# Batch-walking tiles, loads that cast in the DMA, crossbar transposes and a planner with explicit buffers in a fused attention and feed-forward kernel

## Chip, cores and metric

One core of one Trainium2 chip. The metric is the device time of one execution in microseconds. The profile is one execution of the same program, taken on the chip. In the profile PE is the matrix engine (PEld its weight loads), DVE the vector engine, ACT the scalar engine, POOL the GpSimd engine and SP the sync engine, which here only issues DMAs.

## The reference

Attention over 4 batches, 8 heads, 768 positions and head size 64, where a query sees the first 8 keys (global) and the last 96 (local), with a bias linear in the distance. The heads are joined and go through two products with `h - tanh(h)` between them.

```python
scores = q @ k.T / sqrt(64)                      # per batch and head
keep   = (key < 8) | ((0 <= query - key) & (query - key < 96))
dist   = where(global and not local, 96, |query - key|)
a      = softmax(where(keep, scores - slope[h] * dist, -1e9))
x      = (a @ v), heads joined                   # 3072 x 512
h      = x @ w_in                                # 3072 x 2048
out    = (h - tanh(h)) @ w_out                   # 3072 x 512, fp32
```

A tile is 128 query positions of one batch, all heads; there are 24 tiles, six per batch. A tile needs only its own keys, those of the previous tile of its batch, and the 8 global ones, which are copied into unused columns of the previous tile's keys.

## The kernel before

The program first describes every piece of work as an operation with an engine, an estimated duration, what it must come after and which buffers it takes and gives back. A planner then simulates these and emits the instructions of each engine in the order that the simulation found. At run time each engine keeps that order, and semaphores guard the data.

The parts that matter (the cuts are marked):

```python
# tiles u = 0..23 go along batch 0, then batch 1, ...; u // NQ is the batch
def load(u, nm, src, dst):                       # fp32, 256 KB, in rows of 256 bytes
    b, i = u // NQ, u % NQ
    dst[u] = stpool.tile([P, H, Dh], FP32, name=nm)
    started(("ld", nm, u), nc.sync.dma_start(out=dst[u], in_=src[b, :, i*P:(i+1)*P, :]...))
def cast(u, nm, src, dst, eng):                  # POOL (DVE for tile 0): fp32 -> bf16
    dst[u] = bpool.tile([P, H * Dh], BF16, name=nm)
    eng.tensor_copy(out=dst[u], in_=src.pop(u)...)
# ... [cut]
before = [("t", 0), ("t", 1), ("t", 2), ("in", 0), ("t", 3), ("in", 1), ("in", 2), ("in", 3),
          ("out", 0), ("out", 1), ("t", 4), ("out", 2), ("out", 3), ("t", 5)]
for n, it in enumerate(before):                  # loads of tiles wait for loads of weights and the reverse:
    if n >= 2 and (it[0] == "t") != (before[n - 1][0] == "t"):
        gate_of[("ld", "kf", it[1]) if it[0] == "t" else it] = landed(before[n - 2])
# ... [cut]
def a_T(u):                                      # 8 PE transposes of k and q, then a DVE copy
    tr[u] = ps_sm.tile([P, 2, NP, P], BF16, name="sm")
    for j, src in ((1, k_bf), (0, q_bf)):
        for p in range(NP):
            nc.tensor.transpose(tr[u][:, j, p, :], src[u][:, p*P:(p+1)*P], ident)
def a_X(u):                                      # 4 PE transposes of x, then a DVE copy
    ...
groups = [[0, 1], [2, 3], [4, 5]] + [[u, u+1, u+2] for u in range(6, NU, 3)]   # first product
```

The weights come in eight casting DMAs issued by POOL, four quarters of `w_in` and four of `w_out`. PSUM is three pairs of banks (scores and first product) and two single banks (transposes, weighted values, second product).

The softmax here doesn't subtract the row's maximum and nothing guards it: scores larger than these inputs give would overflow.

## Time and profile before

| | before |
|---|---|
| time, median of 2 runs | 243.35 us |
| PE busy, DVE, ACT, POOL | 90%, 60%, 46%, 27% |
| the chain that ended last | PE 85% |
| last weight quarter issued, then to landing | 38.55 us, 7.8 us later (46.4 us) |

This is the profile page of the kernel before: busy time by engine, then the busy share of each engine in 40 equal slices in tenths, the granted PE clock, and the DMA engines.

```profile
span 242.5 us, 4763 instructions
PE 217.6 (90%) x1926; PEld 133.8 (55%) x1952; DVE 144.9 (60%) x274; ACT 111.0 (46%) x137; POOL 66.0 (27%) x111
...
PE   1477867999999979999999999999999999999994
...
PEclk9999799999999999999999999999999999999999
DMA  8997998999999998580991161101100101111112
...
PE 85%; DVE 5%; ACT 3%; DMA 2%; issue 2%; SPq 1%; POOL 1%; ACTq 0%; POOLq 0%
```

One digit of the rows is 6.1 us. PE is full from the eighth digit on, so what can be won lies in the work itself or in the first 45 us, where the DMA row is nearly full: the kernel waits for data.

A busy PE is not a measure of work done, because matmuls overlap and the granted clock changes (0.50 for 3.4 us in the kernel before). So I count the recorded matmuls up to a time and price each with its spacing in warm stretches of the timeline (first product 0.109 us per 256 columns, 0.1625 per 384; second product 0.2165; a transpose 0.0575; a score 0.030; weighted values 0.031). Time minus work done is what PE has lost by then. It is an estimate. Some traces miss up to 29 matmul records, all of the second product and spread evenly, and are scaled up for them; differences below 1 us are not to be read. (The figures here are a recount on which work, losses and the tail add up to the span. The recorded texts below use an earlier count, which has up to 1.2 us more work done by 50 us.)

### The profile page before, as it was taken

How to read it: one execution, taken by the hardware profiler on the slowest of the kernel's cores; microseconds unless marked ns; L12 is line 12 of the kernel's file. 1: busy time of each engine (PE TensorE's matmuls, PEld its weight loads, DVE VectorE, ACT ScalarE, POOL GpSimd, SP SyncE). 2: the span in 40 equal slices, each digit the busy share in tenths (PEclk: the TensorE clock that was granted, in tenths of full speed). 3: DMA queues.
4: the chain of work that ended last, by engine and by line, in shares of the span. 5: the costliest groups of instructions: out<-in, count | busy, mean ns of one | idle time of the engine just before them, and what ended most of it. 6: DMA issues, size and time to landing. Idle time of an engine off the chain costs nothing.

```text
span 242.5 us, 4763 instructions
## 1 busy us (share of the span) xinstructions
PE 217.6 (90%) x1926; PEld 133.8 (55%) x1952; DVE 144.9 (60%) x274; ACT 111.0 (46%) x137; POOL 66.0 (27%) x111
## 2 busy tenths in 40 slices
PE   1477867999999979999999999999999999999994
PEld 1354565655685456646555656665555655555541
DVE  1464474855489558967976677569447866334300
ACT  4443072625257336724862474367325752334310
POOL 5628206156436225432511215130110110000000
PEclk9999799999999999999999999999999999999999
DMA  8997998999999998580991161101100101111112
GB/s 157 218 216 114 203 219 130 217 223 210 260 236 232 207 251 205 97 188 31 221 214 46 35 142 43 43 3 43 44 26 19 46 0 46 45 43 46 43 43 87
DMA packets 82581, 29.66 MB, mean 122 GB/s; under 512 B 75392, under 2 KB 79488, under 8 KB 82560
## 3 DMA queue, kind: packets, MB, share of 16 engines
q1 hardware_dynamic: 78336, 25.17, 47.3%
q0 software_dynamic: 4224, 4.19, 11.0%
q8 instruction: 15, 0.25, 0.4%
q14 instruction: 6, 0.05, 0.1%
HBM read 27.26 MB, written 6.29 MB: 138 GB/s over the span
## 4 chain that ended last, share of the span: by engine, by line
PE 85%; DVE 5%; ACT 3%; DMA 2%; issue 2%; SPq 1%; POOL 1%; ACTq 0%; POOLq 0%
PE big L263 35%; PE op L292 32%; PE big L184 5%; PE sm L172 5%; DMA qf<-in_q_dram 2%; PE sm L207 2%; PE sm L239 2%; DVE g L282 2%; ACT ot L302 1%; PE sm L212 1%; PE sm L292 1%; SPq L147 1%; DVE x L225 1%; ACT th L275 1%; POOL q_bf L160 1%
## 5 line engine op out<-in xcount | busy, mean ns | idle before, releaser
L275 ACT ACTIVATE th<-big 128x768 f32<-128x768 f32 (+1 forms) x60 | 51.3, 855 | 84.9 <-PE big L263 83.8
L282 DVE TENSOR_TENSOR g<-big,th 128x768 bf16<-128x768 f32 (+1 forms) x60 | 60.5, 1009 | 25.0 <-ACT th L275 24.7
L292 PEld LDWEIGHTS <-g 128*128 128x128 bf16 x384 | 34.5, 98 | 35.1 <-issue 1.9
L192 ACT ACTIVATE pd<-big 128x1024 bf16<-128x1024 f32 x24 | 24.5, 1021 | 11.8 <-PE big L184 11.8
L160 POOL CAST k_bf<-kf 128x512 bf16<-128x512 f32 x23 | 16.4, 712 | 36.7 <-PE sm L172 23.3
L263 PE MATMUL big<-xT,w_in_bf_98 128*128 128x384 bf16 (+1 forms) x144 | 24.6, 321 | 0.6 <-DVE xT L246 0.6
L292 PE MATMUL op<-w_out_bf_102,g 128*128 128x512 bf16 x82 | 23.1, 379 | 2.2 <-ACT ot L302 1.5
L263 PE MATMUL big<-xT,w_in_bf_99 128*128 128x384 bf16 (+1 forms) x144 | 24.8, 324 | 0.0
L302 ACT COPY ot<-op 128x512 f32<-128x512 f32 x23 | 13.5, 588 | 24.1 <-PE op L292 22.4
L263 PE MATMUL big<-xT,w_in_bf_100 128*128 128x384 bf16 (+1 forms) x144 | 23.1, 308 | 1.3 <-ACT pd L192 1.3
L292 PE MATMUL op<-w_out_bf_103,g 128*128 128x512 bf16 x88 | 23.1, 379 | 0.2
L176 DVE COPY qk<-sm 128x1024 bf16<-128x1024 bf16 x24 | 16.5, 688 | 11.2 <-PE sm L172 11.1
L263 PE MATMUL big<-xT,w_in_bf_101 128*128 128x384 bf16 (+1 forms) x144 | 23.1, 308 | 0.1
L292 PE MATMUL op<-w_out_bf_105,g 128*128 128x512 bf16 x87 | 22.7, 379 | 0.5 <-issue 0.2
L292 PE MATMUL op<-w_out_bf_104,g 128*128 128x512 bf16 x85 | 22.5, 379 | 0.7 <-issue 0.5
L192 ACT ACTIVATE po<-big 128x1024 bf16<-128x1024 f32 x20 | 20.5, 1026 | 1.5 <-PE big L184 1.5
L224 DVE RECIPROCAL rden<-sm 128x4 f32<-128x4 f32 x40 | 7.2, 180 | 20.9 <-PE sm L212 17.7
L207 PEld LDWEIGHTS <-pd 128*128 128x128 bf16 x192 | 14.6, 101 | 7.7 <-DVE x L225 3.8
L196 DVE TENSOR_TENSOR pd<-pd,mk 128x1024 bf16<-128x1024 bf16 x24 | 17.0, 710 | 2.9 <-ACT pd L192 2.9
L263 PEld LDWEIGHTS <-w_in_bf_98 128*128 128x128 bf16 x144 | 14.1, 102 | 8.1 <-issue 0.9
L263 PEld LDWEIGHTS <-w_in_bf_99 128*128 128x128 bf16 x144 | 14.4, 103 | 6.9
L263 PEld LDWEIGHTS <-w_in_bf_100 128*128 128x128 bf16 x144 | 13.7, 98 | 8.2 <-issue 1.2
(106 smaller groups left out, 250.4 us busy)
## 6 DMA issues: line engine op xcount, KB each, us to landing
kf<-in_k_dram SPq DMA_DIRECT2D x24, 256.0 KB, 4.8
qf<-in_q_dram SPq DMA_DIRECT2D x24, 256.0 KB, 4.9
vf<-in_v_dram SPq DMA_DIRECT2D x24, 256.0 KB, 4.8
out_dram<-ot SPq DMA_DIRECT2D x24, 256.0 KB, 2.1
w_in_bf_98<-in_moe_w_in_dram POOLq DMA_DIRECT2D x1, 512.0 KB, 5.6
w_in_bf_99<-in_moe_w_in_dram POOLq DMA_DIRECT2D x1, 512.0 KB, 5.4
w_in_bf_100<-in_moe_w_in_dram POOLq DMA_DIRECT2D x1, 512.0 KB, 7.3
w_in_bf_101<-in_moe_w_in_dram POOLq DMA_DIRECT2D x1, 512.0 KB, 9.2
```

Of the source, the lines that this page charges most:

```text
L160: eng.tensor_copy(out=dst[u], in_=src.pop(u).rearrange("p h d -> p (h d)"))
L172: nc.tensor.transpose(tr[u][:, j, p, :], src[u][:, p * P : (p + 1) * P], ident)
L176: nc.vector.tensor_copy(out=qk[u], in_=tr.pop(u))
L184: nc.tensor.matmul(s[:, slot(2 * p + hh), :], qk[u - o][r, 1, p, :], qk[u][r, 0, p, :], start=True, stop=True,)
L192: nc.scalar.activation(pr[u, o], s, AF.Exp, bias=0.0, scale=scale)
L196: nc.vector.tensor_tensor(out=pr[u, o], in0=pr[u, o], in1=mk[:, :, m, :], op=ALU.mult)
L207: nc.tensor.matmul(t[:, h, :], pr[u, 0][:, slot(h0 + h), :], vb[u % NV][:, h0 + h, :], start=True, stop=last,)
L263: nc.tensor.matmul(t[:, a, o : o + n], w_in_bf[j][:, c, fo : fo + P], xT[g][:, c, 0:n], start=(c == 0), stop=(c == CD - 1),)
L275: nc.scalar.activation(h_view(ths[g, f0], g), h_view(hs[g, f0], g), AF.Tanh, bias=0.0, scale=1.0)
L282: nc.vector.tensor_tensor(out=dst, in0=h_view(hs.pop((g, f0)), g), in1=h_view(ths.pop((g, f0)), g), op=ALU.subtract,)
L292: nc.tensor.matmul(os_[u], gs[g][:, f, t * P : (t + 1) * P], w_out_bf[f // FJ][:, f % FJ, :], start=(f == 0), stop=(f == CF - 1),)
L302: nc.scalar.copy(out=ots[u], in_=os_.pop(u))
```

## The change

Its intent: take transposes off PE and casts off POOL, and let the first product begin earlier. The core of the diff (cut; the planner and all operations are rewritten):

```diff
+    tiles = [(u % B, u // B) for u in range(NU)]          # batch, position: four batches at each position
+    HEAD = 4
+    NPE = 6
+    groups = [[u] for u in range(HEAD)] + [[u, u + 1] for u in range(HEAD, NU, 2)]
+    bufs["pair"] = [psum.tile([P, 2, BANK], FP32, ...) for i in range(2)]     # scores, weighted values
+    bufs["bank"] = [psum.tile([P, BANK], FP32, ...) for i in range(4)]        # both products, transposes
-        dst[u] = stpool.tile([P, H, Dh], FP32, name=nm)
-        started(("ld", nm, u), nc.sync.dma_start(out=dst[u], in_=...))
+                    pl.op(key, POOL, 0.75, lambda ...: nc.gpsimd.dma_start(out=dst(), in_=rows(src, u)),   # casts
+                          after=[prev and ("issue", prev), ...], take=take, dma=T_LD, ...)
-            if n >= 2 and (it[0] == "t") != (before[n - 1][0] == "t"):
-                gate_of[...] = landed(before[n - 2])
+            if u < NPE:
+                pl.op(("T", nm, u), PE, 0.24, ...)          # as before, on PE
+            else:
+                pl.op(("T", nm, u), SP, 0.6, lambda ...: nc.sync.dma_start_transpose(
+                          out=bufs[nT][got[tT]], in_=buf(nm + "b", (nm + "b", u))), ..., dma=T_TR, lag=0.5)
+        # ... [cut] x is transposed in the same way: PE for u < NPE, the crossbar for the rest
```

All loads but k and q of tile 0 now stand in one queue, POOL's, with the weights between them; the gates are gone. Tile 4 also moved in front of the first two quarters of `w_out`, and the copies of v's global rows went from POOL to DVE.

## The prediction

> **What bounds it now.** The chain of waits is 85% PE (line 263, first product, 35%; line 292, second product, 32%); PE is busy 90% of 242.5 us. PE's work, estimated from warm stretches of the timeline: second product 16 x 0.2165 us per tile, 83 us; first product 83 (0.1625 us per 384 columns, 0.109 per 256); scores 10.6; weighted values 11; k/q transposes 24 x 0.46 = 11; x transposes 24 x 0.23 = 5.5. Sum about 204.5. So 38 us are lost: counting matmuls per stretch, 27 by 60 us, 31 by 100 us, 3.5 in the remaining 139, and 3.6 after the last matmul (eviction 0.59, store 2.1). The early loss is feed: the DMA row is full to 50 us, loads run at about 218 GB/s, a tile's three loads take 3.6 us and a weight quarter 3.2, so six tiles and eight quarters need about 47 us; and the first-product matmuls at 20 us take 200 ns instead of 109.
>
> **What the change does.**
> 1. Removes PE transposes of 18 of 24 tiles: 18 x 0.69 = 12.4 us of PE, on the chain, so most of it counts; and 18 x 1.1 us of DVE copies (DVE is at 60%, off the chain).
> 2. Replaces them with 54 crossbar transposes of 128 KB. No run shows their time. [...] plus issue and 2 us or more to landing, as the page shows for stores. [...] Off the chain in steady state; a wait is likely at the first crossbar tiles (6 to 8).
> 3. k, q, v are cast in the DMA. [...] 70 POOL casts (0.6-0.7 us) go; 70 issues of 1024 short rows come. The weights' issues (512 rows) took 0.75 us; I expect 0.8 to 1.2. POOL was 27% busy. HBM bytes do not fall, so loads still limit the start.
> 4. Batch walk: the first four tiles have no previous tile and pass the first product singly as weight quarters land. By hand, 27-28 us of PE work is done by 50 us, against 24 before: 2-4 us gained, less 1 for 128-column matmuls.
> 5. Evictions go from 768 to 512 columns: tanh 0.6, subtract 0.69 (extrapolated from the trace). ACT and DVE stay near 50-55%. Four single banks hold both products: 2-4 us more stalls.
>
> **Sum.** 193 (PE work) + 23-26 (start) + 3-5 (crossbar hand-over) + 4-6 (steady) + 3.6 (tail) = about 230 us. Range 221 to 240. Chances: faster 0.80, same 0.13, slower 0.07.
>
> **What will show it.** Matmuls of PE transposes down to a quarter; PE busy near 200 us; 95% or more after 80 us; loads 1.1 to 1.3 us apart at the start; the last weight quarter landing near 47-50 us; crossbar transposes landing in 2-4 us; the tail unchanged. The gain should appear mostly after 60 us.
>
> **What would make it wrong.** Cast loads of 256-byte rows much slower than 218 GB/s, or issues on POOL over 1.5 us [...]; crossbar transposes of several us each, blocking stores behind them on SP's in-order queue and so the three output buffers; bank rotation stalling PE. Each pushes to 240 or beyond. If the start packs better than I count, 220.

The sum came to about 230 us (193 + 24.5 + 4 + 5 + 3.6 with the middles of the ranges). The 3-5 us of hand-over, the 2-4 us to landing and "off the chain in steady state" are estimates. That no issue on POOL would take over 1.5 us was likewise an expectation.

## More of the kernel before

The weights as POOL issued them in the kernel before, with two copies that stood in front of them (start, duration, instruction; in brackets the idle time before it, and what ended it):

```profile
10.36 0.89 POOL L153 DMA_DIRECT2D w_in_bf_98<-in_moe_w_in_dram  x1 [0.27 <-DMA vf<-in_v_dram]
...
18.45 0.61 POOL L231 COPY vb_107<-vb_106 8x512 bf16<-8x512 bf16 x1 [4.39 <-PE op L212]
19.01 0.75 POOL L153 DMA_DIRECT2D w_in_bf_99<-in_moe_w_in_dram  x1
...
37.25 0.61 POOL L231 COPY vb_109<-vb_106 8x512 bf16<-8x512 bf16 x1 [10.68 <-PE op L212]
37.81 0.75 POOL L156 DMA_DIRECT2D w_out_bf_104<-in_moe_w_out_dram  x1
38.55 0.75 POOL L156 DMA_DIRECT2D w_out_bf_105<-in_moe_w_out_dram  x1
```

The gaps between them have two causes. One is the waits of one load for another (the gates): the second quarter of `w_in` waited for the first to land, at 15.96 us, and the third of `w_out` for the second, at 34.96. The other is POOL's order: both stood behind a copy of the global rows of v that waited for PE, and left some 3 us after their gates had opened.

## The result, and the profile after

| | before | after |
|---|---|---|
| median, 2 runs | 243.35 us | 230.22 us |
| ratio, fast runs | 1 | 0.945 (0.938 to 0.952) |
| PE's work in all, of the span | 204.5 of 242.5 us | 192.8 of 228.0 us |
| lost by 40 us | 25.6 us | 17.8 us |
| work done / lost by 50 us | 24.1 / 25.9 us | 29.3 / 20.7 us |
| lost by 70 us | 27.5 us | 21.3 us |
| lost by 90 us | 30.4 us | 28.9 us |
| lost by 140 us, 220 us | 33.4, 34.7 us | 30.5, 31.3 us |

A ratio is the mean time of one kernel's fast runs over that of the other's of the same rounds, so it is not quite the ratio of the medians. The predicted 230.0 us was met. The terms of the sum were not, as the table shows: the start lost less than predicted, and 7.6 us went between 70 and 90 us.

The profile page of the changed kernel (same rows as above):

```profile
span 228.0 us, 5127 instructions
PE 207.8 (91%) x2056; PEld 143.3 (63%) x2056; DVE 128.1 (56%) x250; ACT 120.1 (53%) x192; POOL 71.4 (31%) x96
...
PE   1669699789999589999999999999999999999993
...
PEclk9999999999999959999999999999999999999999
DMA  5999999999999999999999999793422321001112
...
PE 87%; DMA 4%; DVE 3%; POOL 2%; ACT 1%; issue 1%; POOLq 0%
```

The PE row has a dent, a 5, in its fourteenth digit (74 to 80 us), and the clock row a 5 in the fifteenth. The weights in the changed kernel's POOL timeline:

```profile
9.46 0.81 POOL L396 DMA_DIRECT2D w_in_bf<-in_moe_w_in_dram  x1
12.80 2.33 POOL L396 DMA_DIRECT2D w_in_bf<-in_moe_w_in_dram  x3
20.00 1.52 POOL L401 DMA_DIRECT2D w_out_bf<-in_moe_w_out_dram  x2
...
28.33 1.54 POOL L401 DMA_DIRECT2D w_out_bf<-in_moe_w_out_dram  x2
```

The last quarter is issued at about 29 us instead of 38.5. The two quarters issued then take 12.2 and 13.6 us to land, with the DMA row at 9 all the while, which is still by 42.8 us instead of 46.4. Tile 5, the last of the first six, landed at 37.5 us instead of 50.0.

The dent, in the chain of waits of the changed kernel (start, duration, what it was):

```profile
72.09 0.97 PE bank L359 x4
...
73.55 0.86 PE bank L359 x4
...
75.49 5.53 DMA xT<-x
81.02 0.04 issue
81.06 4.95 PE bank L340 x24
...
86.50 2.62 PE bank L340 x24
```

Line 340 is the first product, line 359 the second. PE had no product to go on with until the crossbar had landed x of tile 7: 5.5 us from SP's issue. It was not idle: the scores and weighted values of later tiles, some 1.2 us of work at warm spacing, fell into this time. Then 24 matmuls of 256 columns took 4.95 us, 206 ns each, where the next 24 took 2.62 us, 109 ns each. The table of stretches (busy us of each engine and number of instructions, then the granted clock, DMA share, GB/s) says why the first took so long:

```profile
75.50:78.90 3.40, 1.18 (x24) 0.87 (x23) 2.23 (x4) 1.95 (x2) 2.61 (x3) 0.97 1.10 159
78.90:81.00 2.10, 1.29 (x19) 0.89 (x17) 1.50 (x5) 1.18 (x2) 0.88 (x1) 0.50 2.01 122
81.00:86.00 5.00, 4.94 (x29) 3.51 (x29) 2.40 (x4) 2.06 (x3) 0.69 (x1) 0.55 1.36 133
86.50:89.10 2.60, 2.60 (x26) 2.15 (x26) 2.56 (x5) 1.40 (x3) 1.45 (x2) 1.00 1.14 73
```

The granted clock fell to 0.50 at 78.7 us and stayed there for 6.8 us; in the 3.4 us before, PE had been busy for 1.06. The kernel before has one such fall: PE was busy for 1.57 us of the 3.4 from 22.8 us, and the clock was 0.50 for the next 3.4. So the wait costs 5.5 us, less the 1.2 us of work done in it, and the clock another 24 x (206 - 109) ns = 2.3 us: 6.6 of the 7.6 us.

### The profile page after: what moved, and what is told of

Same layout as the page of the kernel before. It is cut to its first block, busy times and chain, and to the rows that moved or that the text cites. A ratio compares the mean times of both kernels' runs of the same rounds, so it can differ in the third digit from the quotient of the medians.

```text
span 228.0 us, 5127 instructions
## 1 busy us (share of the span) xinstructions
PE 207.8 (91%) x2056; PEld 143.3 (63%) x2056; DVE 128.1 (56%) x250; ACT 120.1 (53%) x192; POOL 71.4 (31%) x96
## 4 chain that ended last, share of the span: by engine, by line
PE 87%; DMA 4%; DVE 3%; POOL 2%; ACT 1%; issue 1%; POOLq 0%
PE bank L340 39%; PE bank L359 36%; PE pair L282 5%; PE pair L300 3%; DMA xT<-x 2%; PE pair L302 2%; PE bank L327 2%; DMA qb<-in_q_dram 2%; DVE x L312 1%; DVE pd L291 1%; ACT pd L286 0%; ACT po L286 0%; POOL vb L423 0%; POOL kb L423 0%; DVE xT L272 0%
## 5 line engine op out<-in xcount | busy, mean ns | idle before, releaser
L340 PE MATMUL bank<-xT,w_in_bf 128*128 128x256 bf16 (+1 forms) x896 | 100.1, 263 | 0.2 <-DMA xT<-x 0.2
L359 PE MATMUL bank<-w_out_bf,g 128*128 128x512 bf16 x384 | 95.2, 379 | 0.0
L349 DVE TENSOR_TENSOR g<-bank,th 128x512 bf16<-128x512 f32 x96 | 65.4, 689 | 50.5 <-ACT th L504 50.4
L340 PEld LDWEIGHTS <-w_in_bf 128*128 128x128 bf16 x896 | 77.7, 101 | 18.8 <-issue 0.4
L504 ACT ACTIVATE th<-bank 128x512 f32<-128x512 f32 x96 | 56.9, 600 | 59.1 <-PE bank L340 58.9
L423 POOL DMA_DIRECT2D kb<-in_k_dram x23 | 20.6, 894 | 50.9 <-DMA qT<-qb 24.9
L286 ACT ACTIVATE pd<-pair 128x1024 bf16<-128x1024 f32 x24 | 24.5, 1022 | 18.0 <-PE pair L282 17.9
L423 POOL DMA_DIRECT2D vb<-in_v_dram x24 | 21.5, 897 | 11.1 <-PE pair L282 5.1
L423 POOL DMA_DIRECT2D qb<-in_q_dram x23 | 20.4, 886 | 12.5 <-DMA qT<-qb 5.9
L286 ACT ACTIVATE po<-pair 128x1024 bf16<-128x1024 f32 x20 | 20.4, 1022 | 1.3 <-PE pair L282 1.1
```

The lines of the kernel that those rows point to most:

```text
L286: nc.scalar.activation(buf("po" if o else "pd", ("p", u, o)), t, AF.Exp, bias=0.0, scale=scale)
L340: nc.tensor.matmul(t[:, (f - f0) * n : (f - f0 + 1) * n], w_in_bf[j][:, c, fo : fo + P], xt[:, c, 0:n], start=(c == 0), stop=(c == CD - 1),)
L349: nc.vector.tensor_tensor(out=dst, in0=t.rearrange("q (b n) -> q b n", n=n), in1=th.rearrange("q (b n) -> q b n", n=n), op=ALU.subtract,)
L359: nc.tensor.matmul(o, gg[:, f, t * P : (t + 1) * P], w_out_bf[f // FJ][:, f % FJ, :], start=(f == 0), stop=(f == CF - 1),)
L423: pl.op(key, POOL, 0.75, lambda e, u=u, src=src, dst=dst: nc.gpsimd.dma_start(out=dst(), in_=rows(src, u)), after=[prev and ("issue", prev ...
L504: pl.op(("th", g, f), ACT, 0.55, lambda e, g=g, f=f: nc.scalar.activation(buf("th", ("th", g, f)), buf("bank", ("h", g, f)), AF.Tanh, bias ...
```

## The experiments

Theory A, formed from these two traces: the crossbar saves 12.4 us of PE work and gives 7 or 8 back at the hand-over; the start gains about 6 us because cast loads arrive faster. Rivals: the crossbar is worth nothing net; the start's gain comes from the walk over batches, or from something else in the loading. A kernel's figure below is the median, then the ratio to the kernel before in the same rounds. To set runs against each other I use the ratios. In the call of again, pe24, xpe10 and hw6, two of the seven runs of the kernel before were slow, and the ratios leave them out; the record's verdict on these four, and on gated, is "unclear". Each kernel gave the right result. Where the planner was told something new, it also planned a new order; such an edit is therefore never one instruction alone.

**again: the changed kernel once more.** No edit.

> The changed kernel itself, unchanged, as the yardstick on this chip for the runs beside it. Expected 0.945 of the kernel before (230 us), with the same idle stretch of PE of some 5 us between 75 and 81 us. If it falls outside 0.938 to 0.952 the comparison of the other runs with the first result has to be redone against this one.

230.4 us, 0.946 (0.9405 to 0.9514). The first result holds. The clock record of all four runs is 0.985, as in the first two: the dent is there every time.

**pe24: no crossbar.** Edit: `NPE = 6` becomes `NPE = NU`.

> One part undone: all 24 tiles are transposed on PE (the seventh tile's limit set to 24), everything else kept. Theory A (PE bounds; the crossbar took 18 x 0.69 = 12.4 us of PE work off the chain, and cost about 7.5 us of lost PE time between 70 and 90 us in return, 5.5 of idle and 2.5 of a halved clock): 12.4 more PE work, the 5 to 7 us of hand-over back, so 234 to 237 us. Rival B (the gain came from the start and from the new buffers; the crossbar is worth nothing net): 228 to 231 us. Rival C (the banks that the transposes need now stall the products as well): over 239 us.

236.4 us, 0.973 (0.966 to 0.981). Theory A's number. There is no dent (25.9 us lost by 80 us and 26.5 by 100), and the crossbar's net worth is 0.973 - 0.946, 0.027 of 243.35 us, or 6.6 us: 12.4 less some 6 paid back. (The profiled run is the slowest of the four, 238.6 us; it has a stretch of half clock at 25.5 us that the other three, with a clock record of 1.0, have not.) Rivals B and C fall.

**xpe10: x of tiles 6 to 9 back on PE.** Edit:

```diff
+    NPX = 10
-        if u < NPE:
+        if u < NPX:
             pl.op(("Xt", u), PE, ...
```

> The x transposes of tiles 6 to 9 go back to PE (4 x 0.24 = 1 us of PE work); k and q stay on the crossbar. Theory A (the idle 75 to 81 us is the landing time of the x transposes of tile 7, and the slow stretch after it is the clock that fell in the idle time): the wait on the x transposes before 90 us vanishes, no matmul at half clock there, 223 to 226 us. Rival (the wait only moves to the k and q transposes or to a later tile): 228 to 231 us.

Inconclusive. Five runs went from 224.9 to 231.0 us, two of them slow; the fast ones give 0.926 (0.919 to 0.934). The wait for x before 90 us was gone, as expected, and the three fast runs are faster than the changed kernel; the median of all five, 228.0 us, is hardly so. But the profiled run was a slow one, and there a second stall, on q's transposes, stood between 101 and 114 us. I do not explain the difference of the states from it.

**hw6: the old load path for the first six tiles.** Edit: for u < 6, `nc.sync.dma_start` into fp32 buffers, a cast on POOL (DVE for k and q of tile 0), 12 fp32 buffers instead of 2, and gates by the rule of the kernel before. The order of the loads stays that of the changed kernel, with tile 4 before `w_out`.

> The loads of the first six tiles as in the kernel before: uncast 256 KB loads issued by SP, casts of 0.62 us on POOL, and the same waits of one load for another; all else as in the changed kernel. The changed kernel had done 30.5 us of PE work by 50 us, the kernel before 24.4. Theory A (the earlier start comes from the cast loads, which land 0.87 us apart instead of 1.2): by 50 us about 25 to 27 us of work, total 233 to 236 us. Rival (it comes from the walk over the batches and single tiles): 28 us or more by 50 us, total 229 to 232 us.

236.6 us, 0.972 (0.9665 to 0.977), the total that theory A expected, but not for its reason. The loss by 40 us was 17.0 us, no more than in the changed kernel (17.8); by 50 us it was 23.8, against 20.7 or, in again, 21.2. Uncast loads had not delayed anything; the weights of the second product had, issued at 39.5 us behind the gates. Theory A's explanation of the start was doubtful from here on.

**hw6free: hw6 without the gates.** Edit: no gate is recorded, in the plan or the program.

> As hw6 (first six tiles loaded uncast by SP, cast on POOL), but without the waits of one load for another, in the plan and in the program. In hw6 the work done by 40 us was no less than in the changed kernel, and only then 6 us were lost, waiting for the second product's weights, which were issued at 39.5 us instead of 28 to 29. Theory A2 (the gain at the start is the removal of those waits, not the cast in the DMA): last weight quarter issued before 33 us, 28 us or more of work done by 50 us, 229 to 232 us. Rival (the cast loads' pace is what counts): still 233 us or more.

245.3 us, 1.008 (1.003 to 1.013): a miss of theory A2. The number is in the rival's range, 233 us or more, but not for its reason. The timeline says what I had overlooked. With two queues and no gates, nothing sets the order between them. POOL issued four weight quarters at once at 3.2 us, and SP's loads stood behind them:

```profile
6.15 7.19 SPq L438 DMA_DIRECT2D kf<-in_k_dram  x1
13.38 6.47 SPq L438 DMA_DIRECT2D kf<-in_q_dram  x1
```

SP's six issues before 6 us took 0.45 to 1.17 us each, the seven after that 2.4 to 7.8, and by 40 us PE had done 9.6 us of work, against 22.2 in the changed kernel. The order is thus worth something, and two queues need gates to get it. One queue has it for nothing (in the changed kernel all 78 of POOL's DMAs landed in the order of their issue). That made theory A3.

**gated: gates put back by the old rule, everything else kept.** In one queue a gate holds up all that stands behind it (POOL stood still for 8.6 us up to 28.0 and for 7.2 us up to 39.3, each time before the first load of a tile), and the order of the loads is the new one. Edit (short):

```diff
+    if n >= 2 and (it[0] == "t") != (arrive[n - 1][0] == "t"):
+        gate_of[("ld", "k", it[1]) if it[0] == "t" else it] = landed(arrive[n - 2])
-    pl.op(key, POOL, 0.8, lambda e, j=j: nc.gpsimd.dma_start(...), after=[prev and ("issue", prev)], ...)
+    pl.op(key, POOL, 0.8, lambda e, j=j: started(("out", j), nc.gpsimd.dma_start(...)), after=[gate_of.get(it), ...
```

> The changed kernel with one thing put back: the kernel before's waits of one load for another (the first load of a tile, or the first weight quarter after a tile, waits until the load two places ahead has landed). Loads stay cast and in the one POOL queue. Theory A3 (the gain at the start is that one in-order queue needs no such waits; in hw6 they cost 6 us between 40 and 50 us): last weight quarter issued at 36 us or later instead of 29, 26 to 28 us of work done by 50 us instead of 29.6 to 30.5, total 233 to 237 us. Rival (the waits cost nothing where loads are cast): 229 to 231 us.

239.05 us, 0.981 (0.975 to 0.987): slower than the changed kernel by 0.035 of 243.35 us, 8.5 us, and beyond the range expected. Work by 50 us was 25.3 us. The chain of waits of this run, between 40 and 60 us:

```profile
41.14 0.85 POOL vb L442
41.99 7.87 DMA w_out_bf<-in_moe_w_out_dram
```

The last two quarters of `w_out` left at 42 us and the second product stood until 49.9 us (PE was busy for 2.7 of these 7.9 us). About 6 us of the difference is there by 60 us (26.8 lost, against 20.8 in again). The rest is lost later, mostly between 90 and 100 us, on q's transposes; I did not look for its cause. So the gates are dear in the changed kernel. This is not their price in the kernel before: there the first two quarters of `w_out` left at 21.2 us, here at 30.6, and by 40 us this kernel had lost 19.1 us, the kernel before 25.6.

**nocast: the loads uncast, but in the same queue.** Edit: for u < 6, the DMA lands in fp32 buffers and DVE casts, `copy(e, dst(), buf("kf", ...))`, 0.43 us.

> The first six tiles' loads stay in the POOL queue, in the same order, but land as fp32 and are cast on DVE (0.43 us each). Theory A3 (the cast in the DMA is not what helps; the single queue is): 29 to 30.5 us of work by 50 us, total 229 to 232 us. Rival A (the cast loads are faster in the DMA): loads land 1.1 to 1.2 us apart instead of 0.87, 26 to 28 us of work by 50 us, 233 us or more.

230.7 us, 0.948 (0.943 to 0.953): the changed kernel within noise, 29.5 us of work by 50 us. POOL's issues stood 0.87 to 0.89 us apart, as with the cast. The uncast loads did land more slowly, as rival A said (the first seven in a row 1.27 us apart, 1.12 with the cast; the last weight quarter at 44.7 us instead of 42.8), but PE lost nothing by it. So at the start the cast in the DMA gains nothing in time; the single ungated queue does. Rival A falls. The loads of tiles 6 to 23 were cast in the DMA here too, so what that is worth was not tested.

**seq: the batch walk undone.** Edit:

```diff
-    tiles = [(u % B, u // B) for u in range(NU)]
+    tiles = [(u // NQ, u % NQ) for u in range(NU)]
-        return u - B if tiles[u][1] else None
+        return u - 1 if tiles[u][1] else None
```

and the first tile of a batch is found as `u - tiles[u][1]`.

> The batch walk undone: the tiles go along one batch after the other, as in the kernel before; all else as in the changed kernel. Theory A2 (the walk is a minor part: it spares the first four tiles one score, one exponential and one mask product, and 0.25 us of weighted values each): 1 to 3 us slower, 231 to 234 us, loss by 30 us of 19 to 21 instead of 17.5. Rival (the walk carries the early start): 235 us or more.

228.9 us, 0.941 (0.935 to 0.946): no slower at all. By 30 us it had lost 19.7 us instead of 17.7, as expected, but by 50 us no more than the changed kernel (20.8, against 20.7). What waits for the weights does not gain from earlier tiles. The walk over the batches is worth nothing here. The single-tile groups at the start were kept, so they were not tested.

**lag: one number of the planner.** Edit: `lag=0.5` becomes `lag=3.0` for the crossbar transposes.

> The changed kernel with one number of the planner altered: 3.0 us instead of 0.5 us of extra time from issue to landing of a crossbar transpose. Theory (pe10l's gain of 4 us over the changed kernel is mainly the order: the plan put work behind transposes that had not landed): the idle stretch at 75 us shrinks to 3 us or less, 226 to 228 us. Rival (it is the tiles put back on PE and the buffers): the stretch stays at 5 us, 229 to 231 us.

230.7 us, 0.948 (0.942 to 0.954), and the dent is unchanged (7.5 us lost between 70 and 90 us). The rival holds: telling the planner the truth does not help when it has nothing else to put there.

**xpe10b: xpe10 with deeper k and q buffers.** Edit: `kb` and `qb` 8 buffers instead of 4, `qT` 6 instead of 4.

> As xpe10 (x transposes of tiles 6 to 9 on PE), with 8 instead of 4 buffers for the cast k and q and 6 instead of 4 for the transposed q. xpe10 lost no time before 90 us, but in its profiled run 10 us of the chain between 101 and 114 us were q's transposes, whose loads had waited for a buffer that an earlier transpose still read. Theory (that second stall is the buffer cycle load, transpose, free): no wait on q's or k's transposes of over 2 us after 90 us, 221 to 225 us, and spread of the runs below 1.5%. Rival (the landing time of the transposes in a full DMA is itself the limit): again 225 to 231 us and spread out.

229.4 us, 0.945 (0.9385 to 0.951). The theory falls. Two waits on q's transposes remained, 5.2 us at 91.5 and 8.0 us at 98.9. POOL's in-order queue was now blocked by another buffer, that of v (in brackets the idle time before, and what ended it):

```profile
57.37 0.87 POOL L424 DMA_DIRECT2D qb<-in_q_dram  x1 [0.47 <-DMA vb<-in_v_dram]
77.97 0.87 POOL L424 DMA_DIRECT2D vb<-in_v_dram  x1 [19.72 <-DVE rden L312]
```

After that pause 15 loads were issued in 20 us (78 to 98 us), and the transposes had to land among them.

**pe10l: tiles 0 to 9 wholly on PE.** Edit: `NPE = 10`, the buffers of xpe10b, `lag=3.0`.

> Tiles 0 to 9 wholly on PE (4 x 0.69 = 2.8 us more PE work than the changed kernel), the same larger buffers, and the planner told 2.5 us more from issue to landing of a crossbar transpose, since the trace shows 4 to 5.5 us while loads run. Theory (the hand-over costs what it does because the plan counts on a landing that the trace does not show, and because the crossbar starts while the loads of the coming tiles fill the DMA): no idle time of PE over 1.5 us after 60 us, 222 to 226 us. Rival (the hand-over comes wherever the crossbar starts): an idle stretch of 4 us or more shows up near tile 10, 228 us or more.

225.65 us, 0.929 (0.923 to 0.935), the theory's number and the best version that repeated: faster than both kernels. From 60 us on it lost 3.9 us until 220; the changed kernel lost 10.5. In the page there is no dent:

```profile
span 223.6 us, 5188 instructions
...
PE   1669799779999999999999999999999999999993
...
PEclk9999999999999999999999999999999999999999
```

The plan has work for PE where the changed kernel stood: in the same four stretches between 75.5 and 89.1 us PE was busy throughout (3.40, 2.10, 5.00 and 2.60 us) at a granted clock of 1.00. Alone, the planner's number does nothing (lag), and the buffers with x on PE do not suffice (xpe10b). This points to k and q of tiles 6 to 9 on PE; but it was run only together with the other two edits, so it is not shown.

**pe8lv: earlier hand-over, still deeper buffers.** Edit: pe10l with `NPE = 8` and `vb` 14 instead of 9.

> pe10l with two tiles fewer on PE (8 instead of 10, 1.4 us less PE work) and 14 instead of 9 buffers for v, since in xpe10b the POOL queue stood 19.7 us behind a v load that waited for a buffer. Theory (with deep buffers and the landing time in the plan the hand-over can come earlier): no idle stretch of PE over 1.5 us after 60 us, 223 to 225.5 us, the fastest so far. Rival (tiles 8 and 9 meet a full DMA): an idle stretch near 75 to 85 us, 226 us or more.

227.4 us, 0.935 (0.929 to 0.940): less PE work than pe10l (0.923 to 0.935) and no faster; the theory falls, though not just as the rival had it. The stall came later. Its chain of waits:

```profile
67.83 13.59 DMA vb<-in_v_dram
81.70 0.55 POOL qb L423
82.74 10.00 DMA vb<-in_v_dram
92.74 8.99 DMA qT<-qb
```

With deep buffers POOL issued loads with no pause over 2 us from 42.5 to 91 us, and a transpose of 128 KB issued at 92.7 us took 9.0 us to land. Two things differ from pe10l, so which of them brought the stall is not shown.

## Why the prediction was right

The total was right and the direction too, but errors in its terms cancelled; that the total fits so closely is luck.

- **"18 x 0.69 = 12.4 us of PE, on the chain, so most of it counts."** Right. pe24 shows 6.6 us net, and the loss between 70 and 90 us in the changed kernel (7.6 us) against pe24 (1.8 us) accounts for the rest.
- **"Crossbar hand-over 3-5."** Too small. It was named in the right place (tiles 6 to 8), but measured 5.5 us of wait, with 1.2 us of work in it, plus 2.3 us of halved clock, which I had not counted. Landing took 4.0 to 4.4 us in the median, at or above the top of the predicted 2 to 4. It was 2.4 us after 160 us, when no loads run, and up to 9.0 us in pe8lv.
- **"Start 23-26", from "HBM bytes do not fall, so loads still limit the start" and "the last weight quarter landing near 47-50 us".** Wrong by 2 to 5 us: 20.7 us were lost by 50 us, and the last quarter landed by 42.8. The failing step is in the time of the loads. I counted 3.2 us for a weight quarter; in the kernel before, quarters with no tile between them landed 2.5 to 2.8 us apart (24.4, 27.1, 29.6, 32.4, 35.0 us). Six tiles at 3.6 and eight quarters at 2.6 make an estimate of 42 us instead of 47. What kept the kernel before from this were waits that the diff removes before my eyes: the gates, and POOL's copies. gated shows the gates to be worth 8.5 us in the changed kernel, some 6 of them by 60 us. What made the old start slow stays open in part: by 40 us the kernel before had lost 25.6 us, and no run with one part undone comes near (gated 19.1, hw6 17.0, seq 19.8, nocast 17.7). The single-tile groups, the order of the loads, the copies and the new planner's order were not undone.
- **Point 4, the batch walk as the cause of an earlier start.** Wrong. seq gives the same time without it.
- **Point 3, the cast.** The issue on POOL was right (0.89 us, predicted 0.8 to 1.2). The first loads landed 1.1 us apart, as predicted, behind issues 0.87 us apart. The cast in itself gained nothing for the first six tiles (nocast).
- **"Steady 4-6."** Too large: 2.4 us were lost between 90 and 220 us, so the four single banks cannot cost more than that; tanh took 0.600 us and the subtraction 0.689, as extrapolated.
- **The tail** stayed about as it was, as predicted.

In the sum: start 2 to 5 us better than predicted, steady state 2 to 4 better, hand-over 3 to 5 worse. The terms measured add up to the span, 228.0 us; the time of the run is 1.8 us longer, which the sum had left out. A right total is no proof of its terms.

## What to carry to other kernels

If two queues have to be kept in order, waits for landings cost (between 18 and 42 us gated moved 138 GB/s in the mean, the changed kernel 193), and so does having none (hw6free took 15 us more than the changed kernel). Put the transfers in one queue in the wanted order, as the changed kernel does without a gate. When work moves from a busy engine to a DMA, the gain is real (6.6 us net here, pe24), but the first transfers came while the DMA row stood at 9: the first transpose took 7.0 us to land, against 2.4 after 160 us. Start the hand-over later, so that the busy engine has other work (pe10l, with deeper buffers), and count the clock (2.3 us here, after 3.4 us in which PE was busy for 1.06). Deeper buffers may not be free: in pe8lv a transpose on which the next step waited took 9.0 us to land, after prefetches had been issued up to 91.1 us, though the buffers were not changed alone.

## What the traces show of transposes, issues and the clock

- Transposes: in the changed kernel 128 KB landed in 2.4 us in the median after 160 us (a store of 256 KB in 2.0 us), and between 45 and 110 us, while loads ran, in 4.0 to 5.5 us (medians of q, k and x; 7.4 us at worst), where a plain load of 128 KB took 5.4 to 6.2 us in the median too. One in pe8lv took 9.0 us. An uncrowded transpose held SP's queue for 1.19 us, a store for 0.34 us.
- Issues on POOL in the changed kernel: 0.74 to 0.78 us for a quarter of `w_out` (512 rows), 0.87 to 1.01 us for a tile load (1024 rows; 0.89 in the mean).
- Two queues without an order between them (hw6free): single issues of 7.2, 6.5 and 7.8 us on SP, and 15 us in the total against the changed kernel.
- The clock: in the two traces of the first result the granted clock was 0.50 inside the kernel for 3.4 us (before, from 26.2 us) and 6.8 us (after, from 78.7 us), and 256 columns took 206 ns instead of 109. PE was not idle in the 3.4 us before these falls: its records show it busy for 46% and 31% of them. From 44.6 to 48.0 us of the changed kernel it was busy for 54%, and the clock stayed at 1.00. It came back to 1.00 after 3.4 us with PE busy throughout (26.2 to 29.7 us before, 82.1 to 85.5 after), and did not after 3.4 us with PE busy for 74% (78.7 to 82.1 after).
